# A decode step with two attention layers and two mixers: score halves in one unit's space, a one-tile mixer buffer, the residual stream as columns, and 36 KB of V kept for 24

## The chip, the cores and the metric

The kernel runs on one core of a Trainium2 chip. The metric is the device time of one execution in microseconds, the median of several runs. The core has five engines: TensorE (PE, with its weight loads as PEld), VectorE (DVE), ScalarE (ACT), GpSimd (POOL) and SyncE (SP). Sixteen DMA engines move data between HBM and the core's on-chip memory (128 partitions). SP issues nearly all the large loads here, ACT a few small ones.

## The reference

The input is two sequences of one token, 512 channels. Two layers follow, each an attention block and a mixer block, with the same weights and the same caches in both layers:

```
x = x + A(layernorm(x));  x = x + B(layernorm(x));  x = x + A(layernorm(x));  x = x + B(layernorm(x))

A(x):  q = x @ wq                       # 32 heads of 128, four for each of 8 K/V heads
       p = softmax(q . K / sqrt(128))   # K: (2, 8, 32768, 128) float32
       o = p . V                        # V: same shape
       return o @ wo
B(x):  h = layernorm(x)
       u = gelu(h * w1 + b1)            # one token: every channel to 1792 hidden values
       return u . w2 + b2               # summed over the 1792
```

K and V of a sequence and head are 16 MB each. All 16 pairs are read once in each layer, in float32, because the second layer's q depends on the first layer's output.

## The kernel before

**Units and slots.** A unit is one layer, sequence and K/V head; there are 32, and the four q heads of the group are computed together. A unit's 32768 positions are eight chunks of 4096 (2 MB of K, 2 MB of V). The main loop runs over slots: slot s holds one chunk of K and, ten slots behind (`NCH + LAG`), one chunk of V. In the slots of `PAIRED` two chunks come as one 4 MB load. The order of the work is written out by hand: `pre[s]` runs between a slot's K and V chunks, `post[s]` after the V chunk, each a list filled unit by unit by `at(...)`. Within an engine the instructions run in that order.

**Order of units.** The eight heads of layer 0, sequence 0; three of layer 0, sequence 1; five of layer 1, sequence 0, its head 7 first; then the rest. This gives the mixer of one sequence time while units of the other run.

**Memory.** One tile, `mem`, holds nearly everything: wq of head 0 at its start, a ring of three places for chunks (`RING0`), a region `kept` (`KEPT0`), and the other weights (`home`). In the first 48 slots and from slot 212 on, larger places of 4 MB lie over those that are not yet, or no longer, used. `kept` holds quads of V (four position tiles, 2 KB a partition, 256 KB in all) of head 7. `KEPT = {0: 8, 4: 4}` says that all eight quads of chunk 0 and four of chunk 4 are stored there when layer 0 reads them, and not loaded again when layer 1 reads the same head of the same sequence. `load_v` loads the quads that stay and the rest of their chunk with separate DMAs in layer 0, and only the rest in layer 1.

**Loads.** SP issues x, then wq of head 0, then the chunks in slot order, with other weights between. A load waits on SP until the place it writes has been read; what stands behind it on SP waits too.

**Scores.** `k_chunk` adds four chunks' scores into one PSUM bank, a half of the unit. At the end of each half VectorE transposes it in 32x32 blocks into S (L262) and takes each head's maximum (L263). After the second half `max_1` (L272) and `max_2` (L280) combine the maxima over partitions with two small matmuls, and ScalarE takes the four heads' exponentials over both halves (L290), summing as it goes. `denominators` (L366) sums over partitions on TensorE. `v_chunk` (L328) multiplies the half's exponentials by V into `acc`; `out_1` and `out_2` turn `acc` into rows and multiply by wo. S has two buffers, each of both halves.

**Mixers.** `mix_1` and `mix_2` put the residual stream plus the attention's output on all partitions (`px`) and normalize it into `hx`. `mix_3` makes groups of 2, 4, 4, 4 of the 14 hidden tiles: VectorE forms h * w1 + b1, ScalarE takes gelu over the group, and `mix_3_out` multiplies by w2. `mix_4` adds the residual and, in layer 0, normalizes for the next layer; `to_columns` (L192) turns rows into the columns that `make_q` multiplies by. The residual stream is in `xrow`, one row for each sequence. The mixer of the very last unit has its own code, `last_mixer`, over the freed ring.

**Start.** `xrow` is cleared, x is loaded, normalized and turned, and the first q is made (L612 to L616).

Of the kernel before, what the change touches and what calls it, by code (L numbers as in the profile page):

```python
# [22 lines left out]
KEPT = {0: 8, 4: 4}  # L23
# [4 lines left out]
GELU_GROUPS = (2, 4, 4, 4)  # L28
# [6 lines left out]
def gqa_mixer_kernel(ctx: ExitStack, tc: tile.TileContext, x, kt, v, wq, wo, cols, out):  # L35
# [14 lines left out]
    B, D = x.shape  # L50
# [22 lines left out]
    xrow = const.tile([P, D], F32, name="xrow")  # L73
    nc.vector.memset(xrow, 0.0)
    for b in range(B):
        nc.sync.dma_start(xrow[32 * b : 32 * b + 1, :], x[b : b + 1, :])
# [81 lines left out]
    def layernorm(dst, src):  # L158
        st = work.tile([P, 6], F32, name="ln_st")
        mv = work.tile([P, 2], F32, name="ln_mv")  # L160
        rs = work.tile([P, 1], F32, name="ln_rs")
        nc.vector.bn_stats(st, src)
        nc.vector.bn_aggr(mv, st)
        nc.vector.tensor_scalar_add(rs, mv[:, 1:2], EPS)
        nc.gpsimd.tensor_tensor(rs, rs, half_neg, op=ALU.pow)
        nc.vector.tensor_scalar(dst, src, mv[:, 0:1], rs, op0=ALU.subtract, op1=ALU.mult)
# [14 lines left out]
    xnT = {}  # L181
# [4 lines left out]
    def attention_input():  # L186

        h = row_tile()
        layernorm(h, xrow)
        return h  # L190

    def to_columns(key, h):  # L192

        b = key[1]
        pt = pmisc.tile([P, 512], F32, name="misc")
        for d in range(DT):
            nc.tensor.matmul(
                pt[:, d : d + 1], h[:, d * P : (d + 1) * P], ident[:, 32 * b : 32 * b + 1], start=True, stop=True
            )
        t = const.tile([P, DT], F32, name=f"xnT_{key[0]}_{key[1]}")  # L200
        nc.vector.tensor_copy(t, pt[:, :DT])
        xnT[key] = t
# [23 lines left out]
    sc_ps, S, mx, lsum, oT = {}, {}, {}, {}, {}  # L226
# [13 lines left out]
    def k_chunk(n, c):  # L240

        kc = k_at.pop((n, c))
        half, i = divmod(c, PACK)
        if i == 0:
            sc_ps[n] = pscore.tile([P, 512], F32, name="scores")
        w = CK // (NG * SUB)
        for k in range(SUB):
            at = R * (SUB * i + k)
            q = qpad[n % 2][:, 28 - at : 60 - at]
            for g in range(NG):  # L250
                nc.tensor.matmul(  # L251
                    sc_ps[n][32 * g : 32 * g + 32, :],
                    q,
                    kc[:, (k * NG + g) * w : (k * NG + g + 1) * w],
                    start=(i == 0 and k == 0),
                    stop=(i == PACK - 1 and k == SUB - 1),
                )
        if i == PACK - 1:
            if half == 0:
                S[n] = work.tile([P, HALVES, 512], F32, name="S")  # L260
                mx[n] = work.tile([P, HALVES, R], F32, name="mx")
# [10 lines left out]
    def max_1(n):  # L272
        mxa = work.tile([P, R], F32, name="mxa")
        nc.vector.tensor_reduce(mxa, mx[n].rearrange("p a h -> p h a"), axis=AX.X, op=ALU.max)  # L274
        pm = pmisc.tile([P, 512], F32, name="misc")
        nc.tensor.matmul(pm[:R, :P], mxa, ident, start=True, stop=True)  # L276
        m4[n] = work.tile([R, 1], F32, name="m4")
        nc.vector.tensor_reduce(m4[n], pm[:R, :P], axis=AX.X, op=ALU.max)  # L278

    def max_2(n):  # L280
        pm = pmisc.tile([P, 512], F32, name="misc")
        nc.tensor.matmul(  # L282
            pm[:, :R], m4[n].to_broadcast([R, P]), ident[:R, :R], start=True, stop=True
        )
        neg = work.tile([P, R], F32, name="neg")
        nc.vector.tensor_scalar_mul(neg, pm[:, :R], -SCALE)  # L286
        lsum[n] = work.tile([P, R], F32, name="lsum")
        s = S[n].rearrange("p a (t h) -> p (a t) h", h=R)
# [39 lines left out]
    def v_chunk(n, c):  # L328
# [11 lines left out]
        for q in range(quads):  # L340
            g = q % NG
            col = (c2 * (JT // QT) + q) * 32 + a * R * QT
            nc.tensor.matmul(  # L343
                acc[32 * g : 32 * g + R * QT, :],
                S[n][:, half, col : col + R * QT],
                (own if q < stay else vc)[:, q * w : (q + 1) * w],
                start=(c == 0 and q < NG),
                stop=(c == NCH - 1 and q >= quads - NG),
            )

        for j in range(quads * QT, JT):
            q, t = divmod(j, QT)
            g = j % NG
            col = (c2 * (JT // QT) + q) * 32 + a * R * QT + t * R
            nc.tensor.matmul(
                acc[32 * g : 32 * g + R, :DH],
                S[n][:, half, col : col + R],
                vc[:, j * DH : (j + 1) * DH],
                start=False,
                stop=True,  # L360
                skip_group_check=True,
            )
# [3 lines left out]
    def denominators(n):  # L366
        pl = pmisc.tile([P, 512], F32, name="misc")
        nc.tensor.matmul(pl[:, :R], ones, lsum[n], start=True, stop=True)  # L368
        rl[n] = work.tile([P, R], F32, name="rl")
        nc.vector.reciprocal(rl[n], pl[:, :R])  # L370
# [37 lines left out]
    hx, ysb, px = {}, {}, {}  # L408
# [18 lines left out]
    def mix_2(key):  # L427

        nc.tensor.matmul(px[key], sel1, ysb[key], start=False, stop=True, skip_group_check=True)
        st = work.tile([P, 6], F32, name="ln_st")  # L430
        mv = work.tile([P, 2], F32, name="ln_mv")
        rs = work.tile([P, 1], F32, name="ln_rs")
        nc.vector.bn_stats(st, px[key])
# [9 lines left out]
    def last_mixer(n):  # L443
# [74 lines left out]
        o = work.tile([P, P], F32, name="o", bufs=1)  # L518
# [10 lines left out]
    def mix_3(key, f0, n):  # L529

        u = hidden.tile([P, max(GELU_GROUPS) * D], F32, name="hid")
        hid[key, f0] = u
        for k in range(n):
            f = f0 + k
            nc.vector.tensor_scalar(  # L535
                u[:, k * D : (k + 1) * D],
                hx[key],
                w1c[:, f : f + 1],
                b1c[:, f : f + 1],
                op0=ALU.mult,  # L540
                op1=ALU.add,
            )
        nc.scalar.activation(u[:, : n * D], u[:, : n * D], AF.Gelu_apprx_tanh)  # L543

    def mix_3_out(key, f0, n):
        u = hid[key, f0]
        for k in range(n):
            f = f0 + k
            g = f % NG
            nc.tensor.matmul(  # L550
                rows[key[1]][32 * g : 32 * g + 1, :],
                w2c[:, f : f + 1],
                u[:, k * D : (k + 1) * D],
                start=(f < NG),
                stop=(f >= FT - NG),
            )

    def mix_4(key):
# [4 lines left out]
        r = slice(32 * b, 32 * b + 1)  # L563
        nc.vector.tensor_scalar_add(xrow[r, :], p[r, :], b2c[r, :])
        if layer == LAYERS - 1:
            nc.scalar.dma_start(out[b : b + 1, :], xrow[r, :])
        else:
            hx[layer + 1, b] = attention_input()
# [7 lines left out]
    for n in range(NU):  # L576
# [12 lines left out]
        at(post, s0 + NCH, max_2, n)  # L589
        at(pre, s0 + NCH + 2, denominators, n)  # L590
# [8 lines left out]
        if units[n] == lay[layer, b][-1]:  # L599
# [12 lines left out]
    h0 = attention_input()  # L612
    for b in range(B):
        to_columns((0, b), h0)
# [28 lines left out]
def _layout(A_x, A_k_cache, A_v_cache, A_wq, A_wo, B_w1, B_b1, B_w2, B_b2):  # L643
# [14 lines left out]
        "x": A_x.reshape(B, D),  # L658
# [31 lines left out]
```

## Time and profile before

| | |
|---|---|
| time, median of three runs | 2565.66 us (2565.01 to 2566.82) |
| the profiled execution's own time | 2566.88 us |
| its span, first to last instruction | 2565.1 us |
| bytes moved | 1085.71 MB, 423 GB/s over the span |
| TensorE / VectorE / ScalarE / GpSimd busy | 1665.0 / 215.3 / 136.4 / 4.8 us |
| mean granted TensorE clock | 0.775 |
| chain that ended last: DMA / TensorE | 78% / 21% |

The profile is of one execution. It lists the busy time of each engine, the span in slices with the busy share of the DMA engines, the chain of work that ended last, groups of instructions by source line with what ended the idle time before them, and the DMA issues with the time from issue to landing. L262 is line 262 of the kernel. A group's line reads: line, engine, operation, what it writes <- what it reads, shape; then start and duration in a timeline. The table of stretches gives the same busy times for chosen pieces of the span.

### The profile page before, as it was taken

Reading aid. Unit: us, or ns where it says so; the run is one execution under the profiler, and the core shown is the slowest. Engines: PE = TensorE matmul, PEld = TensorE weight load, DVE = VectorE, ACT = ScalarE, POOL = GpSimd, SP = SyncE. Lnnn points to the kernel's source line nnn. Section 1 sums busy time; section 2 is a strip of 40 time slices with the busy share of each in tenths; the row PEclk is TensorE's granted clock in tenths of the full one; section 3 lists DMA queues with packets and bytes.
Section 4 is the critical chain, followed back from the end, with each engine's and each line's share of the span. In section 5 each row is a group of like instructions: output and inputs, shape, how many; then the busy total and the mean of one; then the engine's idle time right before and its main releaser. Section 6 shows DMA issues by size and latency. Waiting matters only on the chain.

```text
span 2565.1 us, 22227 instructions
## 1 busy us (share of the span) xinstructions
PE 1665.0 (65%) x10208; PEld 494.2 (19%) x10208; DVE 215.3 (8%) x457; ACT 136.4 (5%) x286; POOL 4.8 (0%) x17
## 2 busy tenths in 40 slices
PE   6656665666676666666766766667666656566666
PEld 3111121111121211111212211112112112121212
DVE  1000000000011000000000000001100200000001
ACT  0000000000010000000000000001000100000001
POOL 0000000000000000000000000000000000000000
PEclk8777777777787778777777787778878877777777
DMA  9999999999999999999999999999999999999996
GB/s 409 432 429 430 432 429 430 423 428 425 427 428 425 423 428 425 427 428 427 426 427 424 427 428 427 423 427 428 425 426 427 424 431 432 433 430 430 431 432 267
DMA packets 63612, 1085.71 MB, mean 423 GB/s; under 512 B 7191, under 2 KB 7195, under 8 KB 7582
## 3 DMA queue, kind: packets, MB, share of 16 engines
q1 hardware_dynamic: 63368, 1084.26, 99.2%
q8 instruction: 80, 1.31, 0.2%
q14 instruction: 14, 0.11, 0.0%
q10 hardware_dynamic: 150, 0.03, 0.0%
HBM read 1084.25 MB, written 0.00 MB: 423 GB/s over the span
## 4 chain that ended last, share of the span: by engine, by line
DMA 78%; PE 21%; issue 0%; DVE 0%; ACT 0%; SPq 0%; POOLq 0%; DVEq 0%; ACTq 0%
DMA mem<-in_kt_dram 40%; DMA mem<-in_v_dram 37%; PE acc L343 10%; PE scores L251 9%; PE misc L386 1%; PE misc L216 0%; PE acc L492 0%; PE misc L368 0%; DVE mx L263 0%; ACT S L290 0%; PE rows L550 0%; PE bcast L468 0%; DVE S L262 0%; DVE row L383 0%; PE rows L399 0%
## 5 line engine op out<-in xcount | busy, mean ns | idle before, releaser
L251 PE MATMUL scores<-mem,qpad 128*32 128x512 f32 x4096 | 692.5, 819 | 461.1 <-DMA mem<-in_kt_dram 461.0
L343 PE MATMUL acc<-mem,S 128*16 128x512 f32 x4092 | 694.2, 821 | 391.8 <-DMA mem<-in_v_dram 391.4
L251 PEld LDWEIGHTS scores<-mem,qpad 128*32 128x32 f32 x4096 | 145.1, 135 | 907.8 <-issue 471.6
L343 PEld LDWEIGHTS acc<-mem,S 128*16 128x16 f32 x4092 | 119.6, 115 | 837.6 <-DMA mem<-in_v_dram 529.5
L290 ACT ACTIVATE S<-S,neg 128x256 f32<-128x256 f32 x128 | 94.7, 744 | 2219.2 <-DVE neg L286 2219.2
L216 PEld LDWEIGHTS misc<-xnT,mem 128*128 128x128 f32 x1024 | 141.1, 216 | 119.4 <-issue 119.4
L216 PE MATMUL misc<-xnT,mem 128*128 128x1 f32 x1024 | 149.8, 271 | 0.0
L262 DVE STREAM_TRANSPOSE S<-scores 128x512 f32<-128x512 f32 x64 | 45.9, 717 | 874.5 <-PE scores L251 874.5
L263 DVE TENSOR_REDUCE mx<-S 128x4 f32<-128x512 f32 x64 | 67.4, 1053 | 2.2
L386 PE MATMUL misc<-selg,row 128*128 128x4 f32 x256 | 41.6, 286 | 24.8 <-DVE row L383 24.2
L386 PEld LDWEIGHTS misc<-selg,row 128*128 128x128 f32 x256 | 38.8, 232 | 59.0 <-DVE row L383 32.8
L224 DVE COPY qpad<-misc 128x4 f32<-128x4 f32 x32 | 5.1, 158 | 508.5 <-PE misc L216 508.5
L383 DVE COPY row<-acc 128x512 f32<-128x512 f32 x31 | 21.3, 688 | 192.8 <-PE acc L343 192.8
L399 PE MATMUL rows<-mem,oT 128*1 128x512 f32 x248 | 36.7, 667 | 0.0
L278 DVE TENSOR_REDUCE m<-misc 4x1 f32<-4x128 f32 x32 | 8.9, 279 | 323.1 <-PE misc L276 323.1
L543 ACT ACTIVATE hid<-hid 128x2048 f32<-128x2048 f32 (+1 forms) x12 | 20.4, 1698 | 161.2 <-DVE hid L535 161.2
L535 DVE TENSOR_SCALAR hid<-row,cols_sb 128x512 f32<-128x512 f32 x42 | 20.2, 543 | 53.5 <-PE rows L550 53.4
L290 ACT ACTIVATION_READ_ACCUMULATOR S<-S,neg 128x1 f32 x128 | 24.0, 187 | 0.0
L286 DVE TENSOR_SCALAR neg<-misc 128x4 f32<-128x4 f32 x32 | 5.2, 162 | 181.7 <-PE misc L282 181.7
L276 PE MATMUL misc<-ident,mxa 128*4 128x128 f32 x64 | 14.2, 308 | 7.5 <-DVE mxa L274 7.5
L282 PEld LDWEIGHTS misc<-ident,m 4*128 4x128 f32 x64 | 10.4, 201 | 35.3 <-issue 34.7
L394 DVE TENSOR_TENSOR oT<-misc,rl 128x4 f32<-128x4 f32 x32 | 5.2, 162 | 123.9 <-PE misc L386 123.9
(73 smaller groups left out, 177.1 us busy)
## 6 DMA issues: line engine op xcount, KB each, us to landing
mem<-in_kt_dram SPq DMA_DIRECT2D x164, 2048.0 KB, 11.7
mem<-in_v_dram SPq DMA_DIRECT2D x159, 2048.0 KB, 12.1
mem<-in_kt_dram SPq DMA_DIRECT2D x46, 4096.0 KB, 23.9
mem<-in_v_dram SPq DMA_DIRECT2D x45, 4096.0 KB, 23.6
mem<-in_wq_dram SPq DMA_DIRECT2D x8, 1024.0 KB, 16.9
mem<-in_wo_dram SPq DMA_DIRECT2D x8, 1024.0 KB, 19.2
mem<-in_v_dram SPq DMA_DIRECT2D x7, 1024.0 KB, 12.5
mem<-in_v_dram SPq DMA_DIRECT2D x1, 512.0 KB
```

Of the source, the lines that this page charges most:

```text
L216: nc.tensor.matmul(q_ps[n][:, r : r + 1], wq_sb[h][:, d, r * DH : (r + 1) * DH], xnT[layer, b][:, d : d + 1], start=(d == 0), stop=(d == D ...
L251: nc.tensor.matmul(sc_ps[n][32 * g : 32 * g + 32, :], q, kc[:, (k * NG + g) * w : (k * NG + g + 1) * w], start=(i == 0 and k == 0), stop=( ...
L262: nc.vector.transpose(S[n][:, half, :], sc_ps[n])
L263: nc.vector.tensor_reduce(mx[n][:, half, :], S[n][:, half, :].rearrange("p (t h) -> p h t", h=R), axis=AX.X, op=ALU.max,)
L276: nc.tensor.matmul(pm[:R, :P], mxa, ident, start=True, stop=True)
L290: nc.scalar.activation(s[:, :, h], s[:, :, h], AF.Exp, bias=neg[:, h : h + 1], scale=SCALE, accum_out=lsum[n][:, h : h + 1],)
L343: nc.tensor.matmul(acc[32 * g : 32 * g + R * QT, :], S[n][:, half, col : col + R * QT], (own if q < stay else vc)[:, q * w : (q + 1) * w], ...
L383: nc.vector.tensor_copy(asb, acc)
L386: nc.tensor.matmul(po[:, :R], asb[:, t * DH : (t + 1) * DH], selg[:, t * R : (t + 1) * R], start=(t == 0), stop=(t == QT - 1),)
L399: nc.tensor.matmul(rows[b][32 * r : 32 * r + 1, :], oT[n][:, r : r + 1], wo_sb[h][:, r, :], start=(units[n] == lay[layer, b][0]), stop=(un ...
L535: nc.vector.tensor_scalar(u[:, k * D : (k + 1) * D], hx[key], w1c[:, f : f + 1], b1c[:, f : f + 1], op0=ALU.mult, op1=ALU.add,)
L543: nc.scalar.activation(u[:, : n * D], u[:, : n * D], AF.Gelu_apprx_tanh)
```

## The change

Six edits in one:

1. S becomes two fixed tiles, one for each half, used by every unit. The maximum is taken over the PSUM scores in one value a partition; the transpose of each half waits until the previous unit's last V chunk of that half has been read, and the exponentials are taken half by half, eight instructions of half the length. The denominators add the two halves first.
2. The mixers' hidden tiles use one buffer of 2 KB in place of 8 KB. ScalarE applies scale, bias and gelu to `px` in PSUM in one instruction for each of the 14 tiles; one tile is made every half slot, and the matmul of the tile before goes ahead of it. The mixer ends three slots later.
3. The residual stream is held as columns (`xT`); the row tile `xrow` is gone. `mix_1` and the last mixer add it with matmuls from the columns.
4. x is loaded as columns, 128 rows of 32 bytes, by ACT, and no longer by SP ahead of wq. The first layer norm is done on columns, with two matmuls for the sums (`first_input`).
5. `KEPT` grows from 12 to 18 quads: 36 KB a partition for 24 KB.
6. The last mixer's output uses a ring place in the stead of a tile of its own.

```diff
-KEPT = {0: 8, 4: 4}
+KEPT = {0: 8, 2: 4, 4: 3, 6: 3}
...
-GELU_GROUPS = (2, 4, 4, 4)
...
-    xrow = const.tile([P, D], F32, name="xrow")
-    nc.vector.memset(xrow, 0.0)
-    for b in range(B):
-        nc.sync.dma_start(xrow[32 * b : 32 * b + 1, :], x[b : b + 1, :])
+    xcols = const.tile([P, B, D // P], F32, name="xcols")
+    nc.scalar.dma_start(xcols, x)
...
+    def first_input():
+
+        cen = work.tile([P, B, DT], F32, name="cen", bufs=1)
+        sq = work.tile([P, B, DT], F32, name="sq", bufs=1)
+        m = work.tile([P, B], F32, name="x_m", bufs=1)
+        rs = work.tile([P, B], F32, name="x_rs", bufs=1)
+        p = pmisc.tile([P, 512], F32, name="misc")
+        nc.tensor.matmul(p[:, : B * DT], ones, xcols.rearrange("p b d -> p (b d)"), start=True, stop=True)
+        nc.vector.tensor_reduce(m, p[:, : B * DT].rearrange("p (b d) -> p b d", b=B), axis=AX.X, op=ALU.add)
+        nc.vector.tensor_scalar_mul(m, m, 1.0 / D)
+        for b in range(B):
+            nc.vector.tensor_scalar_sub(cen[:, b, :], xcols[:, b, :], m[:, b : b + 1])
+        nc.vector.tensor_mul(sq, cen, cen)
+        p = pmisc.tile([P, 512], F32, name="misc")
+        nc.tensor.matmul(p[:, : B * DT], ones, sq.rearrange("p b d -> p (b d)"), start=True, stop=True)
+        nc.vector.tensor_reduce(rs, p[:, : B * DT].rearrange("p (b d) -> p b d", b=B), axis=AX.X, op=ALU.add)
+        nc.vector.tensor_scalar(rs, rs, 1.0 / D, EPS, op0=ALU.mult, op1=ALU.add)
+        nc.gpsimd.tensor_tensor(rs, rs, half_neg.to_broadcast([P, B]), op=ALU.pow)
+        for b in range(B):
+            xT[b] = xcols[:, b, :]
+            xnT[0, b] = const.tile([P, DT], F32, name=f"xnT_0_{b}")
+            nc.vector.tensor_scalar_mul(xnT[0, b], cen[:, b, :], rs[:, b : b + 1])
...
-    def to_columns(key, h):
-
-        b = key[1]
+    def to_columns(key):
+
+        layer, b = key
         pt = pmisc.tile([P, 512], F32, name="misc")
         for d in range(DT):
             nc.tensor.matmul(
-                pt[:, d : d + 1], h[:, d * P : (d + 1) * P], ident[:, 32 * b : 32 * b + 1], start=True, stop=True
-            )
...
+                pt[:, d : d + 1], ysb[key][:, d * P : (d + 1) * P], ident[:, :1], start=True, stop=True
+            )
+        xT[b] = const.tile([P, DT], F32, name=f"xT_{layer}_{b}")
+        nc.vector.tensor_scalar_add(xT[b], pt[:, :DT], b2c)
...
+        nc.vector.tensor_scalar(
+            xnT[layer + 1, b], pt[:, :DT], mv[:, 0:1], rs, op0=ALU.subtract, op1=ALU.mult
+        )
...
+    S = [const.tile([P, 512], F32, name=f"S{k}") for k in range(HALVES)]
...
-            nc.vector.transpose(S[n][:, half, :], sc_ps[n])
-            nc.vector.tensor_reduce(
-                mx[n][:, half, :],
-                S[n][:, half, :].rearrange("p (t h) -> p h t", h=R),
-                axis=AX.X,
-                op=ALU.max,
-            )
+                mx[n] = work.tile([P, HALVES], F32, name="mx")
+            nc.vector.tensor_reduce(mx[n][:, half : half + 1], sc_ps[n, half], axis=AX.X, op=ALU.max)
...
+    def turn_scores(n, half):
+        nc.vector.transpose(S[half], sc_ps[n, half])
+
+    def exponentials(n, half):
+        s = S[half].rearrange("p (t h) -> p t h", h=R)
         for h in range(R):
             nc.scalar.activation(
                 s[:, :, h],
                 s[:, :, h],
                 AF.Exp,
-                bias=neg[:, h : h + 1],
+                bias=neg[n][:, h : h + 1],
                 scale=SCALE,
-                accum_out=lsum[n][:, h : h + 1],
+                accum_out=lsum[n][:, half, h : h + 1],
             )
...
+        both = work.tile([P, R], F32, name="both")
+        nc.vector.tensor_add(both, lsum[n][:, 0, :], lsum[n][:, 1, :])
+        nc.tensor.matmul(pl[:, :R], ones, both, start=True, stop=True)
...
-        mine = ident[:, 32 * b : 32 * b + 1].to_broadcast([P, P])
-        nc.tensor.matmul(px[key], mine, xrow, start=True, stop=False, skip_group_check=True)
+        for d in range(DT):
+            nc.tensor.matmul(
+                px[key][:, d * P : (d + 1) * P],
+                xT[b][:, d : d + 1].to_broadcast([P, P]),
+                ident,
+                start=(d == 0),
+                stop=False,
+                skip_group_check=True,
+            )
...
-        hx[key] = row_tile()
-        nc.vector.tensor_scalar(hx[key], px[key], mv[:, 0:1], rs, op0=ALU.subtract, op1=ALU.mult)
+        nc.vector.tensor_scalar_mul(off, mv[:, 0:1], -1.0)
+        nc.vector.tensor_scalar_mul(slope[key], w1c, rs)
+        nc.vector.scalar_tensor_tensor(shift[key], slope[key], off, b1c, op0=ALU.mult, op1=ALU.add)
...
-            nc.tensor.matmul(to, ident[:, 32 * b : 32 * b + 1], xrow[:, c], start=True, stop=False, skip_group_check=True)
+            nc.tensor.matmul(to, xT[b][:, g : g + 1], ident, start=True, stop=False, skip_group_check=True)
...
+    def hidden_tile(key, f):
+
+        if f:
+            g = (f - 1) % NG
             nc.tensor.matmul(
                 rows[key[1]][32 * g : 32 * g + 1, :],
...
+                w2c[:, f - 1 : f],
+                hid[key, f - 1],
+                start=(f <= NG),
+                stop=(f > FT - NG),
+            )
+        if f < FT:
+            hid[key, f] = hidden.tile([P, D], F32, name="hid")
+            nc.scalar.activation(
+                hid[key, f],
+                px[key],
+                AF.Gelu_apprx_tanh,
+                bias=shift[key][:, f : f + 1],
+                scale=slope[key][:, f : f + 1],
             )
...
+        at(post, s0 + NCH, exponentials, n, 0)
+        at(post, s0 + NCH // 2 + LAG - 1, turn_scores, n, 0)
+        at(post, s0 + NCH + LAG - 1, turn_scores, n, 1)
+        at(post, s0 + NCH + LAG - 1, exponentials, n, 1)
...
-            for k, w in enumerate(GELU_GROUPS):
-                at(pre, e + 2 + k, mix_3, key, sum(GELU_GROUPS[:k]), w)
-                at(post, e + 2 + k, mix_3_out, key, sum(GELU_GROUPS[:k]), w)
-            at(post, e + 5, take_rows, key)
-            at(pre, e + 6, mix_4, key)
+            for f in range(FT + 1):
+                k, v_side = divmod(f + 1, 2)
+                at(post if v_side else pre, e + 1 + k, hidden_tile, key, f)
+            at(post, e + 8, take_rows, key)
+            at(pre, e + 9, mix_4, key)
             if layer + 1 < LAYERS:
-                at(pre, e + 7, lambda k: to_columns(k, hx[k]), (layer + 1, b))
+                at(pre, e + 10, to_columns, key)
...
-        "x": A_x.reshape(B, D),
+        "x": np.ascontiguousarray(A_x.reshape(B * (D // P), P).T),
```

More of the change, by code (lines that the diff above doesn't have):

```diff
@@ L224, in make_q @@
             nc.vector.tensor_copy(qpad[n % 2][:, 28 : 28 + R], q_ps[n][:, :R])
-    sc_ps, S, mx, lsum, oT = {}, {}, {}, {}, {}
+    sc_ps, mx, lsum, oT = {}, {}, {}, {}
+    S = [const.tile([P, 512], F32, name=f"S{k}") for k in range(HALVES)]
     k_at, v_at = {}, {}
@@ L244, in k_chunk @@
         if i == 0:
-            sc_ps[n] = pscore.tile([P, 512], F32, name="scores")
+            sc_ps[n, half] = pscore.tile([P, 512], F32, name="scores")
         w = CK // (NG * SUB)
@@ L251, in k_chunk @@
                 nc.tensor.matmul(
-                    sc_ps[n][32 * g : 32 * g + 32, :],
+                    sc_ps[n, half][32 * g : 32 * g + 32, :],
                     q,
@@ L344, in v_chunk @@
                 acc[32 * g : 32 * g + R * QT, :],
-                S[n][:, half, col : col + R * QT],
+                S[half][:, col : col + R * QT],
                 (own if q < stay else vc)[:, q * w : (q + 1) * w],
@@ L356, in v_chunk @@
                 acc[32 * g : 32 * g + R, :DH],
-                S[n][:, half, col : col + R],
+                S[half][:, col : col + R],
                 vc[:, j * DH : (j + 1) * DH],
@@ L406, in out_2 @@
             )
-    hx, ysb, px = {}, {}, {}
+    ysb, px = {}, {}
+    slope, shift, stats = {}, {}, {}
     def take_rows(key):
@@ L432, in mix_2 @@
         rs = work.tile([P, 1], F32, name="ln_rs")
+        off = work.tile([P, 1], F32, name="off", bufs=1)
+        slope[key] = work.tile([P, FT], F32, name="scale", bufs=1)
+        shift[key] = work.tile([P, FT], F32, name="bias", bufs=1)
         nc.vector.bn_stats(st, px[key])
@@ L517, in last_mixer @@
         assert f0 == FT
-        o = work.tile([P, P], F32, name="o", bufs=1)
+        o = tiles[FT][:, :P]
         nc.vector.tensor_scalar_add(o, res, b2c)
@@ L527, in gqa_mixer_kernel @@
     hid = {}
[L529 to L549, printed above, removed]
+    def hidden_tile(key, f):
+        if f:
+            g = (f - 1) % NG
             nc.tensor.matmul(
                 rows[key[1]][32 * g : 32 * g + 1, :],
[L552 to L555, printed above, removed]
+                w2c[:, f - 1 : f],
[11 more added lines that the diff above has]
+                scale=slope[key][:, f : f + 1],
             )
@@ L562, in mix_4 @@
         nc.tensor.matmul(p, sel1, ysb[key], start=False, stop=True, skip_group_check=True)
-        r = slice(32 * b, 32 * b + 1)
-        nc.vector.tensor_scalar_add(xrow[r, :], p[r, :], b2c[r, :])
+        ysb[key] = row_tile()
         if layer == LAYERS - 1:
-            nc.scalar.dma_start(out[b : b + 1, :], xrow[r, :])
-        else:
-            hx[layer + 1, b] = attention_input()
+            nc.vector.tensor_scalar_add(ysb[key], p, b2c)
+            nc.scalar.dma_start(out[b : b + 1, :], ysb[key][:1, :])
+        else:
+            nc.vector.tensor_copy(ysb[key], p)
+            st = work.tile([P, 6], F32, name="ln_st")
+            mv = work.tile([P, 2], F32, name="ln_mv")
+            rs = work.tile([P, 1], F32, name="ln_rs")
+            nc.vector.bn_stats(st, p)
+            nc.vector.bn_aggr(mv, st)
+            nc.vector.tensor_scalar_add(rs, mv[:, 1:2], EPS)
+            nc.gpsimd.tensor_tensor(rs, rs, half_neg, op=ALU.pow)
+            stats[key] = mv, rs
     pre, post = {}, {}
```

50 lines of the change are left out of this document (15 added, 35 removed).

## The prediction

> **What bounds the kernel now.** I read the page from the top: busy shares, slices, DMA queues, the chain that ended last, DMA issues.
>
> ```profile
> span 2565.1 us, 22227 instructions
> PE 1665.0 (65%) x10208; PEld 494.2 (19%) x10208; DVE 215.3 (8%) x457; ACT 136.4 (5%) x286; POOL 4.8 (0%) x17
> ...
> DMA  9999999999999999999999999999999999999996
> ...
> DMA packets 63612, 1085.71 MB, mean 423 GB/s; under 512 B 7191, under 2 KB 7195, under 8 KB 7582
> ...
> DMA 78%; PE 21%; issue 0%; DVE 0%; ACT 0%; SPq 0%; POOLq 0%; DVEq 0%; ACTq 0%
> ...
> mem<-in_kt_dram SPq DMA_DIRECT2D x164, 2048.0 KB, 11.7
> mem<-in_v_dram SPq DMA_DIRECT2D x159, 2048.0 KB, 12.1
> ```
>
> TensorE is busy 65% and nothing else comes near. The DMA row is full in every slice but the last (the tail after the last byte), so the end comes from bytes over a rate. The PE 21% in the chain is no second bound: a load is issued when TensorE frees its place, and then stands in a queue. The last two lines show that: a 2 MB load lands 11.7 to 12.1 us after its issue.
>
> Next, the table of stretches: the start, the stage of 2 MB loads, the stage of 4 MB loads, and 128 us that hold three 1 MB loads (columns: length, busy time and count of the five engines, granted clock, DMA share, GB/s).
>
> ```profile
> 0.00:64.00 64.00, 40.29 (x236) 20.68 (x240) 7.92 (x18) 1.28 (x1) 1.51 (x11) 0.87 0.96 410
> 832.00:1600.00 768.00, 504.86 (x3064) 146.08 (x3056) 53.38 (x110) 30.59 (x80) 0.00 (x0) 0.78 1.01 427
> 2048.00:2496.00 448.00, 277.08 (x1736) 86.20 (x1736) 30.27 (x63) 15.04 (x40) 0.00 (x0) 0.77 1.00 431
> 600.00:728.00 128.00, 84.22 (x499) 22.87 (x498) 8.61 (x18) 7.37 (x17) 0.00 (x0) 0.77 1.01 427
> ```
>
> 2 MB (2,097,152 bytes) at 427 GB/s is 4.91 us, 4 MB at 431 is 9.73. Two of the first less one of the second is 0.09 us, the price of one more load in a full queue. What is left, 4.82 us for 2 MB, is 435 GB/s for bytes alone. The last row, with its 1 MB loads, runs at the same 427.
>
> How late may TensorE be before the DMA starves? A 2 MB load lands 11.7 us after issue and moves in 4.9, so 6.8 us of other bytes lie ahead of it. The first wq load (1 MB, 2.4 us of bytes) landed 5.0 us after issue, so starting takes up to 2.6 us. The reserve is 6.8 - 2.6 = 4.2 us in each round.
>
> Last, the timeline, at the start and where one head's V ends.
>
> ```profile
> 0.74 0.39 ACTq L128 DMA_DIRECT2D cols_sb<-in_cols_dram  x1
> 0.91 0.48 DVE L74 MEMSET xrow<- 128x512 f32 x1 [0.91 <-PEq L676]
> ...
> 1.43 0.61 SPq L76 DMA_DIRECT2D xrow<-in_x_dram  x2
> ...
> 2.08 0.36 SPq L99 DMA_DIRECT2D mem<-in_wq_dram  x1
> ...
> 16.91 6.38 PE L251 MATMUL scores<-mem,qpad 128*32 128x512 f32 x32 [0.79 <-DMA mem<-in_kt_dram]
> ```
>
> ```profile
> 957.56 3.50 PE L343 MATMUL acc<-mem,S 128*16 128x512 f32 x16 [2.98 <-DMA mem<-in_v_dram]
> ...
> 962.44 1.92 PE L251 MATMUL scores<-mem,qpad 128*32 128x512 f32 x16 [1.38 <-DMA mem<-in_kt_dram]
> ...
> 965.21 0.36 PE L368 MATMUL misc<-lsum,one 128*128 128x4 f32 x2
> ```
>
> The first shows SP, the queue of the big loads, standing behind a memset and two loads of x until 2.08. The second is the one place where an exponential could hold TensorE: the denominators (L368) come 965.21 - 961.06 = 4.1 us after the V chunk before them ends.
>
> **The change, part by part.**
>
> *V that stays.* A quad is 2 KB a partition, 256 KB. Kept are 18 quads in place of 12, and each is spared once for each of two sequences in the second layer: 2 x 6 x 262,144 = 3.146 MB of 1085.71. At 435 GB/s that is 7.23 us (at the mean 427: 7.37). I take 7.23, because fixed costs are counted apart. It lies on the path, since the queue never empties.
>
> *More, smaller loads.* Head 7 of layer 0 goes from 9 V loads to 11, twice; in layer 1 it stays at 7. Four more loads at 0.09: +0.36. From below, the last row of the table shows no price: 0. From above, a load that finds an empty queue costs 2.6 each, +10.4. I take 0.36, the row of queued loads; 10.4 is a rival. A shorter load also shortens the reserve: with 1.25 MB (3.0 us) in place of 4.9 it is 2.3 us, with 1 MB (2.4 us) it is 1.7; before has 1 MB there too (chunk 4), at 427.
> The Trainium skill (DMA: Bandwidth & Descriptors, Anatomy of one DMA) speaks against this edit: it fits a DMA as 2.0 us fixed plus bytes over 436e3. By that the four loads would be an estimated +8.0 and the whole change -0.6; the measured 0.09 in a queue disagrees for overlapped loads.
>
> *The start.* SP loses the memset wait and two x issues. The wq load can issue when the ACT queue does today, at 0.74 instead of 2.08: -1.34 on everything behind it in a full queue. x becomes 128 rows of 32 bytes on ACT ahead of cols; the 144 packets of that queue took 0.6% of 16 x 30 us, 20 ns each, so 126 more rows cost 0.16 us of one engine, 0.01 of 16. The chain to the first q grows: two small matmuls (0.36 each), about nine small DVE operations (0.15 to 0.18), one POOL power (0.55), some 3.5 us with the hops, against 5.7 for the statistics and turns of before. With x landed by 5, q stands near 15.5, when the first K (1.34 earlier than 16.9) lands. A late x is covered: wq, two 4 MB loads, wq again and a third keep the DMA busy until about 36 us, and only the first K chunk pair (6.4 us) must be done some 3 us before. So q may come as late as 26. Bounds: -1.34 to 0; I take -1.34, the issue rows.
>
> *Scores.* The maximum is taken from PSUM (its row today 1.05), the transpose (0.717) moves behind the last V chunk that reads the half, and four exponentials of 256 become eight of 128, each between half and all of 0.742. At the boundary one half's chain is 0.72 + 4 x (0.38 to 0.77) + an add of 0.16 + hops: 2.5 to 4.1 us. TensorE gets there 4.1 us after the same start, so its wait is near 0, below the reserve. Queued on DVE behind the transpose is the copy of acc (0.69), which waits for the same V chunk; TensorE needs it 3.2 us later. On ACT nothing behind is due. The score bank is free two slots before it is written again. Cost 0.
>
> *Mixers (three; the last has its own code).* DVE drops 14 operations of 0.54 and one of 0.81. ACT does 14 of 512: from 1.06 for 1024 and 1.91 for 2048, 0.63 each, 8.9 in place of 6.8. Four more table loads of 1.28 fall between, since exponentials now cut into the groups. With one buffer each matmul waits for the activation issued half a slot (about 4.9 us) before, and each activation for the matmul just ahead. At the worst spot (two slots before the end) activation, table load and half the exponentials stand in series before the denominators: 0.7 + 0.63 + 1.28 + 4.1 = 6.7 against 4.1 plus some 1.5 of other TensorE work: about 1 us late of a reserve of 4.2. Result columns come three slots later, at the slot where the next layer's first q reads them, after a V chunk of 1.9 us that covers two DVE operations. mix_1 turns from two to eight matmul passes (up to 1.2 us more), covered by TensorE's waits for DMA. The queue instructions of SP pass none of these. Cost 0; with cover gone, see the rivals.
>
> *Tail.* The last mixer swaps stationary and moving operand of the residual (0.62 us for eight) and takes another place for o: 0.
>
> Sum: -7.23 + 0.36 - 1.34 = -8.2. The profiled execution took 2566.88 (span 2565.1 and 1.8 around it) and becomes 2558.7; it is 1.2 above the median of 2565.66, on which the forecast is 2557.5 us, 0.32% faster. About 0.2% (5.1 us) can be told from no change.
>
> **The rivals.**
> - *The start gives nothing*, because x or wq starts later than ACT's slot shows: -6.9, 2558.8. For it: no SP issue earlier than 1.43 is on record. Against: its wait there is for the memset.
> - *Cut loads drain the queue*: +10.4 in place of 0.36 gives +1.8, 2567.5. Against: 427 GB/s around the 1 MB loads. The skill's fit would give an estimated 2565.1.
> - *Mixers starve the DMA*: were all four table loads (5.1), two activations (1.3) and both halves' exponentials (6.2) in series, 12.6 less 4.1 and 4.2 is 4.3 us, three times: 13 - 8.2 = +4.8, 2570.5. Against: the slots spread them over 10 us each.
> - *Slower: the late half holds every head.* Place: the denominators behind the second half's transpose and exponentials. TensorE waits, frees K and V late, the queue runs dry. It decides from a chain of 4.1 + 4.2 = 8.3 us; at 8.8 it costs 32 x 0.5 = 16 us, +7.8, 2573.5. For it: 32 repeats of a short overrun are enough. Against: the chain adds up to half of that.
>
> **How the numbers follow.** Forecast 0.74; start gives nothing 0.10; drained queue 0.05; mixers 0.04; late half 0.07. The first two are faster (0.84), the next two within 0.2% (0.09), the last slower (0.07). The forecast's own range is 2556 to 2560 (best terms -7.37 and -1.34 with runs 1 us apart; worst -6.8 and the same). The 8 in 10 range is 2555.5 to 2561.5: it takes in the second case and a lost microsecond or two in the mixers.
>
> **What would show it.** 1082.6 MB in the queue line; 427 and 431 unchanged in their stages; wq issued near 0.74; a DMA row of 9s with the mixers' windows not below about 422; L368's successor waiting for an activation under a microsecond; the same 22 us from the last V piece to the end. The prediction is wrong if the GB/s of the 2 MB stage falls by more than 1, if DMA share dips at heads' boundaries, or if the start's first 64 us move fewer bytes than 410 GB/s.

## The result and the profile after

The changed kernel takes 2559.66 us (median of 8 runs, 2557.59 to 2561.61), the kernel before 2566.57 us (median of 8 runs beside it, 2565.01 to 2569.33). The ratio is 0.9971, 95% interval 0.9960 to 0.9982: 4.6 to 10.3 us faster. The forecast of 2557.5 us (0.32% faster) was 2.2 us low, inside its range of 2555.5 to 2561.5. The profiled execution took 2560.44 us, span 2558.7: 6.4 us less span than before.

The page of the changed kernel, the lines that answer to those shown of before:

```profile
span 2558.7 us, 22602 instructions
...
DMA  9999999999999999999999999999999999999996
...
DMA packets 64330, 1082.58 MB, mean 423 GB/s; under 512 B 7397, under 2 KB 7401, under 8 KB 8298
...
DMA 75%; PE 24%; issue 1%; DVE 0%; ACT 0%; POOLq 0%; DVEq 0%; ACTq 0%
```

3.13 MB less is moved at the same mean rate, the DMA row still full, and the chain is still DMA. The same four stretches as before (the start, 2 MB loads, 4 MB loads, and 128 us with 1 MB loads then and cut ones now):

```profile
0.00:64.00 64.00, 40.24 (x228) 18.58 (x229) 5.66 (x19) 1.28 (x1) 1.67 (x11) 0.84 0.98 418
832.00:1600.00 768.00, 506.20 (x3072) 147.51 (x3068) 45.63 (x120) 42.91 (x160) 0.00 (x0) 0.78 1.01 426
2048.00:2496.00 448.00, 291.68 (x1742) 86.43 (x1742) 26.15 (x68) 23.67 (x83) 0.00 (x0) 0.74 1.00 431
600.00:728.00 128.00, 84.63 (x498) 23.59 (x490) 8.03 (x20) 9.74 (x33) 0.00 (x0) 0.78 1.01 427
```

The first 64 us move 418 GB/s in place of 410. The stage of 2 MB loads, which holds the first re-read of head 7, lost 1 GB/s. The start in the timeline:

```profile
0.73 0.41 ACTq L73 DMA_DIRECT2D xcols<-in_x_dram  x1
...
0.74 0.41 SPq L96 DMA_DIRECT2D mem<-in_wq_dram  x1
...
5.21 0.57 PE L162 MATMUL misc<-xcols,one 128*128 128x8 f32 x2 [5.21 <-DMA xcols<-in_x_dram]
...
16.05 0.16 DVE L232 COPY qpad<-misc 128x4 f32<-128x4 f32 x1 [6.96 <-PE misc L224]
16.32 6.59 PE L262 MATMUL scores<-mem,qpad 128*32 128x512 f32 x32 [0.30 <-issue]
```

wq is issued at 0.74 (before: 2.08), x lands by 5.21, q is ready at 16.05. From the groups and the waits, what the moved vector and scalar work costs and who waits for it:

```profile
L299 ACT ACTIVATE S<-S,neg 128x128 f32<-128x128 f32 x256 | 130.5, 514 | 2127.4 <-DVE neg L290 1985.0
...
L272 DVE TENSOR_REDUCE mx<-scores 128x1 f32<-128x512 f32 x64 | 44.3, 692 | 527.1 <-PE scores L262 527.1
...
L566 ACT ACTIVATE hid<-bcast,bias,scale 128x512 f32<-128x512 f32 x42 | 32.7, 778 | 177.2 <-PE rows L557 136.5
```

```profile
PE misc L379 <- DVE both L378: 12.8, 32, 2.1
```

The last line (total, times, longest) is the denominators waiting for the late half's exponentials: 0.4 us a unit, 2.1 at most.

**Where the 6.4 us came from.** The trace has every DMA packet with its end. Adding packets up in the order of the loads gives the moment at which each load's bytes are there, and the lead of one kernel over another at equal loads. All times are counted from the first instruction of each span. The lead over the kernel before, in us, at the K load of some slots (head 7's V is read again in slots 98 to 105 and 202 to 209; two executions of the changed kernel, the second described below):

```
slot of the K load      4     48     96    108    172    200    212    252
changed kernel       1.03   1.04   1.24   4.16   4.68   4.31   7.12   7.38
changed, again       1.28   1.21   0.78   2.01   2.70   2.03   5.06   5.09
undo_kept            1.23   1.21   1.49   1.32   1.44   1.23   1.55   1.82
start_only           1.44   1.35   1.14   1.31   1.39   1.18   1.14   1.20
```

There is a head start of 1.0 to 1.4 us, two steps where V is not loaded again, and little else. All rows use the same single execution of the kernel before, so each step carries some tenths of its chance as well. Of the 7.4 us at the last K loads, 6.8 are left when the last V piece is multiplied (2543.14 in the kernel before, 2536.39 here) and 6.4 at the end:

```profile
2543.14 1.04 PE L343 MATMUL acc<-mem,S 128*16 128x512 f32 x4 [0.20 <-DMA mem<-in_v_dram]
```

```profile
2536.39 1.04 PE L352 MATMUL acc<-mem,S 128*16 128x512 f32 x4 [0.22 <-DMA mem<-in_v_dram]
```

### The profile page after: what moved, and what is told of

It reads as the page before. It is cut to its first block, busy times and chain, and to the rows that moved or that the text cites. A ratio compares the mean times of both kernels' runs of the same rounds, so it can differ in the third digit from the quotient of the medians.

```text
span 2558.7 us, 22602 instructions
## 1 busy us (share of the span) xinstructions
PE 1684.1 (66%) x10220; PEld 504.8 (20%) x10220; DVE 169.2 (7%) x455; ACT 201.7 (8%) x584; POOL 4.9 (0%) x17
## 4 chain that ended last, share of the span: by engine, by line
DMA 75%; PE 24%; issue 1%; DVE 0%; ACT 0%; POOLq 0%; DVEq 0%; ACTq 0%
DMA mem<-in_kt_dram 37%; DMA mem<-in_v_dram 37%; PE acc L352 11%; PE scores L262 10%; PE misc L224 1%; PE misc L397 0%; PE rows L410 0%; PE acc L516 0%; DMA xcols<-in_x_dram 0%; PE misc L379 0%; ACT S L299 0%; PE bcast L492 0%; PE rows L557 0%; ACT mem L526 0%; ACT mem L537 0%
## 5 line engine op out<-in xcount | busy, mean ns | idle before, releaser
L299 ACT ACTIVATE S<-S,neg 128x128 f32<-128x128 f32 x256 | 130.5, 514 | 2127.4 <-DVE neg L290 1985.0
L272 DVE TENSOR_REDUCE mx<-scores 128x1 f32<-128x512 f32 x64 | 44.3, 692 | 527.1 <-PE scores L262 527.1
L557 PE MATMUL rows<-hid,cols_sb 128*1 128x512 f32 x84 | 49.8, 679 | 0.0
L299 ACT ACTIVATION_READ_ACCUMULATOR S<-S,neg 128x1 f32 x256 | 47.9, 187 | 0.0
L566 ACT ACTIVATE hid<-bcast,bias,scale 128x512 f32<-128x512 f32 x42 | 32.7, 778 | 177.2 <-PE rows L557 136.5
L282 DVE TENSOR_REDUCE m<-misc 1x4 f32<-1x128 f32 x32 | 8.9, 279 | 377.3 <-PE misc L280 377.3
L379 PE MATMUL misc<-both,one 128*128 128x4 f32 x64 | 14.3, 294 | 12.8 <-DVE both L378 12.8
L288 PEld LDWEIGHTS misc<-m,one 1*128 1x128 f32 x64 | 10.8, 209 | 36.3 <-issue 35.7
L379 PEld LDWEIGHTS misc<-both,one 128*128 128x128 f32 x64 | 11.5, 225 | 16.4 <-DVE both L378 14.5
L557 PEld LDWEIGHTS rows<-hid,cols_sb 128*1 128x1 f32 x84 | 8.0, 96 | 32.6 <-issue 29.9
```

The source lines that it names most:

```text
L272: nc.vector.tensor_reduce(mx[n][:, half : half + 1], sc_ps[n, half], axis=AX.X, op=ALU.max)
L299: nc.scalar.activation(s[:, :, h], s[:, :, h], AF.Exp, bias=neg[n][:, h : h + 1], scale=SCALE, accum_out=lsum[n][:, half, h : h + 1],)
L379: nc.tensor.matmul(pl[:, :R], ones, both, start=True, stop=True)
L557: nc.tensor.matmul(rows[key[1]][32 * g : 32 * g + 1, :], w2c[:, f - 1 : f], hid[key, f - 1], start=(f <= NG), stop=(f > FT - NG),)
L566: nc.scalar.activation(hid[key, f], px[key], AF.Gelu_apprx_tanh, bias=shift[key][:, f : f + 1], scale=slope[key][:, f : f + 1],)
```

## Experiments

All times are against runs of the kernel before on the same chip. Theory at the outset: bytes and the start make the whole difference, and what is missing of each step (2.9 us in place of the 3.6 us that 1.5 MB of bytes take) goes at cut loads. Rivals: the compute edits hold or free the queue; a head start is absorbed by the ring.

**The changed kernel again** (no edit), as yardstick.

> The changed kernel itself, as the yardstick beside the three others on the same chip. Both theories: 6 to 8 us under the kernel before (ratio 0.997); the lead in the landing of equal loads steps up by about 2.9 us at each of the two re-reads of head 7 and is about 1 us elsewhere.

2560.0 us, ratio 0.9970 (0.9960 to 0.9981). The steps were 1.2 and 3.0 us: the first re-read came out 1.7 us worse than in the first profile, with nothing changed. The first re-read varies from one execution to the next.

**V kept as before.**

```diff
-KEPT = {0: 8, 2: 4, 4: 3, 6: 3}
+KEPT = {0: 8, 4: 4}
```

> The changed kernel with 12 quads of V kept, as before. Theory (bytes are what the change gains, the rest of the compute edits costs nothing): only the start is left, 0.8 to 1.4 us under the kernel before, no step in the lead at the re-reads of head 7. Rival (the halves and mixers themselves free the queue or hold it): a drift of the lead along the 32 units, up or down by over 1 us, and a total away from that.

2567.58 us, ratio 1.0003 (0.9994 to 1.0012). Without the six quads the gain is gone: the bytes carry it. The expected head start (ratio 0.9996) lies inside the interval, and the lead in its profile stays between 0.9 and 2.0 us from end to end, without a step. There is no lasting drift from the halves or the mixers.

**The start alone**, in the kernel before.

```diff
-        nc.sync.dma_start(xrow[32 * b : 32 * b + 1, :], x[b : b + 1, :])
+        nc.scalar.dma_start(xrow[32 * b : 32 * b + 1, :], x[b : b + 1, :])
```

> The kernel before with one edit: the two x rows are issued by ACT in place of SP. Theory: wq is issued near 0.75 us in place of 2.08 and every load lands 1.2 to 1.3 us earlier to the end: 0.8 to 1.4 us under the kernel before. Rival (a head start is absorbed by the ring of buffers): the lead is there in the first loads and gone by the last, total 0.

2566.12 us, ratio 0.9997 (0.9988 to 1.0005): too small to time. In the timeline of its start:

```profile
0.74 0.41 SPq L99 DMA_DIRECT2D mem<-in_wq_dram  x1
...
1.43 0.78 ACTq L76 DMA_DIRECT2D xrow<-in_x_dram  x2
...
10.25 0.69 DVE L162 BATCH_NORM_STATS2 ln_st<-xrow 128x6 f32<-128x512 f32 x1 [6.98 <-DMA xrow<-in_x_dram]
...
23.13 0.16 DVE L224 COPY qpad<-misc 128x4 f32<-128x4 f32 x1 [6.67 <-PE misc L216]
```

wq goes out at 0.74 as expected, and the lead stays at 1.1 to 1.4 us to the last K loads, so a head start is not absorbed. The K load of slot 98, which the prediction shows for the kernel before at 962.44, is used here at 961.30, and one of the last K loads at 2465.12 in place of 2466.52 (this run's two lines, then that of the kernel before):

```profile
961.30 1.92 PE L251 MATMUL scores<-mem,qpad 128*32 128x512 f32 x16 [1.57 <-DMA mem<-in_kt_dram]
...
2465.12 5.34 PE L251 MATMUL scores<-mem,qpad 128*32 128x512 f32 x32 [3.62 <-DMA mem<-in_kt_dram]
```

```profile
2466.52 3.64 PE L251 MATMUL scores<-mem,qpad 128*32 128x512 f32 x32 [1.41 <-DMA mem<-in_kt_dram]
```

That is about the 1.34 us by which the issue moved. q was ready only at 23.13, 7 us later than before. x is issued at 1.43 in both kernels, but here wq and two K loads are issued before or beside it, and the statistics wait for x until 10.25 (3.28 before). Nothing was lost by that: the late-x cover of the prediction held.

**The same quads with whole chunks.**

```diff
-KEPT = {0: 8, 2: 4, 4: 3, 6: 3}
+KEPT = {0: 8, 2: 8, 4: 2}
```

> The changed kernel with the same 18 quads cut otherwise: chunks 0 and 2 whole, two quads of chunk 4, so one cut load in each re-read in place of three, and two fewer loads where the quads are first read. Theory (the missing 0.7 us of each re-read is lost at cut loads, whose shorter bytes leave the queue shorter than TensorE is late): each re-read spares 3.3 to 3.6 us in place of 2.9, total 0.8 to 1.6 us under the changed kernel. Rival (the rate, not the cuts): the re-reads spare 2.9 again, total within 0.3 us of the changed kernel. Second rival (a chunk left out whole lets two K loads meet and costs more): slower than the changed kernel.

2558.51 us, ratio 0.9970 (0.9958 to 0.9981); steps 2.6 and 3.2 us. Not the 3.3 to 3.6 expected: one cut load in place of three did not bring the missing part back. In the first re-read some 1.4 us of the lead went in slots 97 to 100, which have no cut load at all here.

**The quads spread, and bunched.** Second theory: in a slot that has little V to load, TensorE's own work (two chunks, the previous head's output and wo, the denominators) is longer than the loads, and the ring of three places runs dry.

```diff
-KEPT = {0: 8, 2: 4, 4: 3, 6: 3}
+KEPT = {1: 5, 3: 4, 5: 5, 7: 4}            # spread
+KEPT = {0: 8, 1: 8, 2: 2}                  # bunched, and bunched again
```

> The changed kernel with its 18 quads in chunks 1, 3, 5, 7 (5, 4, 5, 4), so four cut loads in each re-read, none left out whole, and none in the slot that also holds the previous head's output, denominators and wo. Theory (in a slot that has little to load TensorE's own work of that slot, 7 to 10 us by its clock, is the longer one, and the ring of three places runs dry): steps of the lead at the re-reads 3.2 to 4.2 us, total 1 to 2.5 us under the changed kernel. Rival (each cut load costs by itself, 0.3 us or more): steps of 2.9 or less, total the same as the changed kernel or above it.

> The same 18 quads in chunks 0, 1 (whole) and 2 (two quads): one cut load in each re-read, but two slots running without a V load. Theory (TensorE is the longer one there): two slots and the outputs take TensorE 15 to 20 us against 9.8 us of K loads and a reserve of about 4: 1 to 6 us lost in each re-read, steps 0 to 2.5, total 2 to 8 us over the changed kernel. Rival (cut loads cost): one cut in place of three, steps 3.3 or more, total under the changed kernel.

Spread: 2561.82 us, ratio 0.9980 (0.9971 to 0.9990), steps 2.0 and 2.7, as the rival said and not as the theory did. Bunched: 2559.41 us, ratio 0.9968 (0.9954 to 0.9981), steps 4.0 and 4.3, the opposite of what the theory expected. That pointed back to cut loads as the cost, so the two that follow ask for it with the fewest and the most cuts:

> The kernel of the run bunched once more, timed with more rounds beside the changed kernel's earlier runs. Theory (a chunk left out whole takes no place in the ring and costs nothing; a cut load takes a whole place for fewer bytes and costs 0.2 to 1.2 us): the two re-reads spare 3.5 us or more each, no slot of theirs loses over 0.3 us, total 0.5 to 2 us under the changed kernel. Rival (the first look at bunched had luck with the granted clock): a slot with little to load loses over 1 us in this profile, total the same as the changed kernel.

> The same 18 quads over all eight chunks (3, 2, 2, 2, 2, 2, 2, 3), so eight cut loads in each re-read and none left out whole. Theory (price by the cut, 0.25 to 0.45 us for loads of 1.25 to 1.5 MB): each re-read loses 2 to 4 us over its bytes and spares 1 to 2.5; eight more loads where the quads are read first cost about 1 us: total 2 to 5 us over the changed kernel. Rival (only a TensorE that is slow in a slot with less than 1.5 chunks costs): each re-read spares 3.5 or more, total within 1 us of the changed kernel.

```diff
-KEPT = {0: 8, 2: 4, 4: 3, 6: 3}
+KEPT = {0: 3, 1: 2, 2: 2, 3: 2, 4: 2, 5: 2, 6: 2, 7: 3}     # eight_cuts
```

Bunched again: 2559.83 us, ratio 0.9969 (0.9957 to 0.9981), steps 0.9 and 3.3. Eight cuts: 2559.55 us, ratio 0.9970 (0.9959 to 0.9981), steps 2.8 and 3.6. Eight cut loads cost no more than three, and the layout with one lost most of a step the second time. A price by the cut falls. The two executions of the one bunched kernel differ by more than the layouts do. Both stretches begin at the K chunk of the first slot without V (columns as before; the last three are granted clock, DMA share, GB/s). First execution:

```profile
960.00:970.00 10.00, 8.28 (x74) 3.12 (x78) 2.08 (x6) 2.17 (x8) 0.00 (x0) 1.00 1.01 426
970.00:980.00 10.00, 7.05 (x56) 2.24 (x52) 0.19 (x1) 0.00 (x0) 0.00 (x0) 0.99 1.01 425
```

Second execution:

```profile
960.00:970.00 10.00, 8.32 (x42) 3.43 (x46) 0.41 (x3) 1.42 (x6) 0.00 (x0) 0.60 1.00 426
970.00:980.00 10.00, 10.00 (x84) 2.95 (x76) 0.69 (x1) 0.00 (x0) 0.00 (x0) 0.89 0.74 285
```

And the timelines there, TensorE's kept V chunk between two load issues of SP. First execution:

```profile
963.38 0.33 SPq L332 DMA_DIRECT2D mem<-in_v_dram  x1
...
964.94 1.91 PE L352 MATMUL acc<-mem,S 128*16 128x512 f32 x16
...
969.49 0.33 SPq L247 DMA_DIRECT2D mem<-in_kt_dram  x1
```

Second execution:

```profile
964.46 0.33 SPq L332 DMA_DIRECT2D mem<-in_v_dram  x1
...
967.07 3.62 PE L352 MATMUL acc<-mem,S 128*16 128x512 f32 x16
...
974.17 0.33 SPq L247 DMA_DIRECT2D mem<-in_kt_dram  x1
```

With a granted clock of 1.00 the kept chunk took 1.91 us and the next place of the ring came free 6.1 us after the last; DMA stayed at 426. With 0.60 it took 3.62, everything before and after it stretched too, and the next issue came 9.7 us after the last: DMA fell to 285 GB/s, and the loads of slot 100 came 3.6 us later than their bytes ask for. The changed kernel has the same pair: granted 0.86 in the 16 us from 960 with DMA share 1.00 in its first profile, 0.68 with 0.93 in the second, whose step is the small one:

```profile
960.00:976.00 16.00, 11.09 (x86) 3.32 (x82) 2.40 (x6) 2.14 (x8) 0.00 (x0) 0.86 1.00 419
```

```profile
960.00:976.00 16.00, 13.91 (x82) 4.56 (x82) 1.30 (x5) 1.82 (x8) 0.00 (x0) 0.68 0.93 384
```

So the second theory had a mechanism that these traces show, a TensorE that takes longer than the little that is left to load, and the wrong sizes: the clock granted there moved the steps more than the layout did. In the same 16 us from 960, three of the nine first re-reads with 18 quads had a granted clock under 0.70 (changed again 0.68, whole chunks 0.66, bunched again 0.68); their steps are 1.2, 2.6 and 0.9 us. The other six had 0.86 to 1.00, and steps of 2.0 to 4.0, mean 3.0. No run set the clock, so its part is observed and not tested, and the 2.6 and the 2.0 show that it isn't all. What takes the 0.7 us in the first profile of the changed kernel, with the DMA share at 1.00, stays open.

Over the nine layouts and repeats with 18 quads the 18 steps lie between 0.9 and 4.3 us, mean 2.8. Those above 3.6 are more than the bytes can give, which is the chance of the one execution that they are measured against and of their own. All of the nine but the spread one (0.9980) have ratios of 0.9968 to 0.9971, and the intervals of all overlap.

**A longer chain before the late exponentials.** Idle activations on a small tile of their own, before the second half's exponentials in every unit:

```diff
+    idle = const.tile([P, 32], F32, name="idle")
+    nc.vector.memset(idle, 0.0)
+    def delay():
+        for _ in range(16):        # chain_48: 48
+            nc.scalar.activation(idle, idle, AF.Copy)
...
+        at(post, s0 + NCH + LAG - 1, delay)
         at(post, s0 + NCH + LAG - 1, exponentials, n, 1)
```

> The changed kernel with 16 small activations (some 3.5 us) ahead of the second half's exponentials in all 32 units. Theory (TensorE comes to the denominators 4 us after the V chunk, and the queue holds 4.2 us more): no more than 2 us longer in total. Rival (each microsecond past TensorE's arrival holds the DMA): 2 us in each of 32 units, 64 us longer.

> The same with 48 activations (some 10.5 us). Theory: past the reserve by 2 to 5 us in the 21 units with 2 MB loads, hidden in the 11 units with 4 MB loads: 40 to 105 us longer. Rival without a reserve: 6 to 9 us in 32 units, 190 us or more. Should it be within 10 us of the changed kernel, the reserve is far above 4.2.

chain_16: 2558.54 us, ratio 0.9970 (0.9959 to 0.9982), no cost. But TensorE hardly waits for the longer chain: its wait at the denominators is 18.1 us over 30 waits in all (12.8 over 32 in the changed kernel), 6.1 of it in the last unit. So the 3.7 us of idle work (16 activations of 0.228) is hidden before TensorE arrives, and this run says nothing yet of the reserve in the queue:

```profile
PE misc L386 <- DVE both L385: 18.1, 30, 6.1
```

chain_48: 2590.32 us in one run, about 31 us over the changed kernel. That is below the 40 to 105 expected, and it comes from other places: the lead is lost at the three mixers (7.9, 8.7 and 10.7 us) and a little in the first re-read (some 2.5 us), not at the plain units. In a stretch of plain units the rate is whole, although the idle work is there (75 us of ACT):

```profile
1216.00:1600.00 384.00, 247.88 (x1518) 70.76 (x1518) 22.59 (x59) 75.24 (x320) 0.00 (x0) 0.80 1.01 427
```

In that stretch the denominators' matmuls wait 2.6 us each for the exponentials, 3.3 at most (total, times, longest; the view of waits for this stretch). At each mixer they wait 9.3 us (one line of the timeline; then the 10 us at that mixer):

```profile
PE misc L386 <- DVE both L385: 13.0, 5, 3.3
```

```profile
817.98 0.59 PE L386 MATMUL misc<-both,one 128*128 128x4 f32 x2 [9.30 <-DVE both L385]
```

```profile
810.00:820.00 10.00, 2.02 (x10) 0.82 (x14) 0.35 (x2) 9.41 (x29) 0.00 (x0) 0.53 0.57 244
```

Among 2 MB loads 3.3 us late costs nothing and 9.3 us late starves the DMA. The estimated reserve of 4.2 us lies between the two; the runs don't place it closer. Among 4 MB loads, from 2100 to 2480 us, waits of up to 6.5 us cost nothing. What was mis-sized in the expectation is how late 11.0 us of idle work (48 activations of 0.229) makes TensorE.

**No gelu in the three mixers.**

```diff
-                AF.Gelu_apprx_tanh,
+                AF.Identity,
```

> The changed kernel with the identity in place of gelu in the three mixers with 14 single tiles (their values are left without the gelu), so no table is loaded between them and the exponentials. Theory (mixers lie within the reserve): the total stays within 1 us of the changed kernel, and the stretches of the three mixers keep their GB/s. Rival (table loads hold the late half of the scores and so the loads): 1 to 3 us shorter.

2558.92 us, ratio 0.9969 (0.9957 to 0.9981), 0.7 us under the changed kernel's median and inside the spread of its runs: the table loads between gelu and exponentials (18 fewer here, 1.28 us each) cost nothing that can be measured.

## Why the prediction was right, point by point

- **V that stays, -7.23 us, and smaller loads, +0.36.** Right that this is the change: undo_kept takes the gain away. The size was too good. Together the two terms gave -6.9 for two re-reads; the first profile shows steps of 2.9 and 2.8 us, and the mean over 18 is 2.8: -5.7. The mis-sized step is "it lies on the path, since the queue never empties". In a slot without V the queue can empty, because TensorE's work in it stays: the DMA share at that boundary of heads was 0.93 in the second profile and 0.74 in bunched again. The prediction worked out that a short load cuts the reserve to 1.7 to 2.3 us, and then took from the 427 GB/s of a 128 us stretch that this has no price; that stretch holds the first reads, where the kept quads do load. The shortfall of 1.2 us is about what the whole fell short: -6.9 between the medians in place of -8.2. The range left room for "a lost microsecond or two in the mixers"; it was lost in the re-reads. (The rest of the 2.2 us to the forecast is the median of the kernel before, 0.9 us higher in the later runs.)
- **Its own signs of being wrong.** A dip of the DMA share at heads' boundaries was one, and it came where head 7 is read again. A fall of the 2 MB stage by more than 1 GB/s was another: from 427 it went to 426 in the first profile and to 425 in the second. Both point at the same step.

```profile
832.00:1600.00 768.00, 509.54 (x3076) 148.51 (x3068) 45.66 (x120) 42.55 (x160) 0.00 (x0) 0.78 1.00 425
```

- **The price of an added load.** 0.09 us is not contradicted: eight_cuts has twelve loads more than the changed kernel and the same time, to some 3 us. The Trainium skill's fit, given for DMAs that GpSimd issues, of 2.0 us fixed for each (DMA: Bandwidth & Descriptors, Anatomy of one DMA) would give an estimated 24 us for them; issued by SP and queued behind others, they showed none of it.
- **The start, -1.34.** Right. The issue moved by exactly that, the second K load was consumed 1.2 us earlier, and at slots 4 and 48 the lead was 1.0 to 1.4 us in all profiles with this start. It is read from the landing of loads; the times alone can't show it. q at 16.05 answers the 15.5 of the text.
- **Scores at 0.** Right. The half's exponentials take 0.514 each, inside 0.38 to 0.77, and the wait at the denominators is 0.4 us a unit. chain_16 lengthened the chain by 3.7 us without effect.
- **Mixers at 0.** Right as to time: the 80 us around each of the three move 427, 424 and 426 GB/s, 426 each before. One activation takes 0.778 us and not the 0.63 taken from wider ones. A row of the same form stood in the profile before, the last mixer's 128x512 gelu with scale and bias at L502, 0.805 us, and would have given the better estimate. The cover was large enough. chain_48 shows that of all places this one has the least of it.
- **Tail at 0.** 22.3 us from the last V piece's matmuls to the end, 22.0 before.
- **The rivals.** "Cut loads drain the queue" had part of the truth, at some 0.75 us a re-read in place of 2.6 us an added load, and with TensorE's clock rather than the load's size as what went with it. "The late half holds every head" was put at a chain of 8.3 us; 3.7 us more were free, and 11.0 us more cost at the mixers and in the first re-read, not at the plain units.

## What to carry to other kernels

In this kernel bytes spared under a full DMA queue were worth their time only where the engine that frees the buffers needed less time for that stretch than the bytes that remained. So price each spared load against the consumer's work in the same slot, at the slowest clock that the profile shows there. An average rate over a long stretch hides such a place; the landing of equal loads in two traces shows it. A wait on another engine was free here as long as the queued loads covered it (3.3 us among 2 MB loads, not 9.3), so ask how many microseconds lie in the queue and not whether there is a wait.

## What the runs showed of the hardware

- The same program in the same 10 us was granted a TensorE clock of 1.00 in one execution and 0.60 in another; 16 matmuls of one V chunk then took 1.91 and 3.62 us. In this DMA-bound kernel the loads of that slot came 3.6 us late in the second, at the place where the reserve was thin.
- A single gelu of 128x512 with scale and bias tiles took 0.778 us read from PSUM and 0.805 us read from SBUF (L502 before); in place in SBUF without them, 128x1024 took 1.06 us and 128x2048 1.91 us.
- Repeats of one kernel lie some 4 us apart (2557.59 to 2561.61 for the changed one), so one microsecond is read from the landing of loads and not from times.
